# VectorE and GpSimd in program order through the whole second stage, and a verdict read back one block later

## The chip, the cores and the metric

The kernel runs on one core of a Trainium2 chip. A core has five engines that work side by side, each with its own queue of instructions: TensorE (PE, matrix multiplies), VectorE (DVE), ScalarE (ACT), GpSimd (POOL) and SyncE (SP, which issues most of the DMAs here). They wait for one another through semaphores. The metric is the device time of one execution in microseconds (us), as a median over runs; lower is better.

## The reference

A gated linear attention over 768 positions gives rows of 384 features for 3072 tokens. Two MLPs follow, and only they matter for the change:

```
x = rmsnorm(attention(q, k, v, a_re, a_im)) * rms_g     # 3072 x 384
u = silu(x @ w_gate) * (x @ w_val)                      # d_ff 1536
x = u @ w_out1                                          # 384
h = x @ w_in                                            # d_ff 2048
out = (h * clip(h + 3, 0, 6) / 6) @ w_out2              # 384
```

The inputs and outputs are 32-bit floats. The weights come as 64-bit numbers, which the kernel turns into 32-bit ones itself.

## The kernel before

Every float32 product is made of three matmuls in a reduced format: each operand is split into a high and a low part, and high x high, high x low and low x high are added in PSUM. Helper `mm3` issues them (its three lines are L735 to L737), so matmuls of all layers carry these lines, and the tile names tell them apart. VectorE makes the low parts (a subtraction), ScalarE the high parts (a copy).

**First stage** (to about 577 us). Attention and the first layer (`w_gate`, `w_val`), in units. Five engines follow an order written out by hand. The results `u` go to DRAM (`u_dr`).

**Second stage** (from about 577 us). Six blocks of 512 tokens. For each block n there are two parts:

- `o1[n]`, the product with w_out1: 12 steps j. A step fetches `uu` from DRAM (`fetch`, L898, three buffers), splits it into `uh` (ScalarE, L904) and `ul` (VectorE, L905; two buffers each) in `part`, and does 9 matmuls into the three PSUM tiles `po` (`gemm`). Three matmuls of a step need `uh` alone. After the last step `evict` copies the three `po` to `x2h` (ScalarE, L918) and makes `x2l` (VectorE, L919); both are named `x2b` in the profile.
- `m2[n]`, the second MLP: 16 steps j. `up` does 9 matmuls into one of two PSUM tiles `ph`. `act` then runs ScalarE (L948, `r`), VectorE (L949, `r`; it reads `ph` for the last time), ScalarE (L950, `gh`), VectorE (L951, `gl`). `down` does 9 matmuls into `po`, two steps behind `up`. At the end `evict` copies the three `po` to `ob`, the middle one on VectorE (L964), and SP stores them.

Beside that, the weights of the second stage are decoded tile by tile (44 tiles in all; 24 of them run beside blocks 0 and 1). Each takes four VectorE operations (L301, L303, L305 and a range check, L311, which keeps the smallest magnitude in `wmin`), one of ScalarE and one of GpSimd (L788).

The kernel is exact only for numbers in a certain range. So `recheck` reads the gate weights again (24 tiles `rawc`, two buffers, a DMA on SP each) and range-checks them (L311), and `verdict` gathers all flags with seven small VectorE operations (`okt`, `okc`), sends 128 numbers to DRAM and reads them back as one row (`okr`, two DMAs on SP, L1015 and L1016), and reduces that row to one bit (`badf`, `badi`; L1017 and L1018). At the very end the bit decides whether a slow fallback runs.

**The order.** A planner orders the instructions of each engine by a model of their times, from the program's order as priority. A `manual_schedule` context takes the named engines out of that: they keep the program's order among the instructions of the context. `manB` is such a context for VectorE and GpSimd; it opens in front of the second stage and is closed after block 0 (`o1[0]`, `o1[1]`, `m2[0]` and the decoding, merged by hand with `run`). Everything after it (blocks 1 to 5, the range checks of `recheck`, `verdict`) is ordered by the planner on all engines, and it may also mix its instructions in between those of `manB`. The loop over blocks, which emits o1[n+1] and then m2[n]:

```
for n in range(NB):
    seq = m2[n][0] + do(m2[n][1]) if n else []
    if 1 <= n and n + 1 < NB:
        seq = do(o1[n + 1][0]) + o1[n + 1][1] + do(o1[n + 1][2]) + seq
    run((seq, 0, 1), ([...recheck(i)...] if n in (1, 2) else [], 0, 1))
    if n == 3:
        verdict()
```

The two lists of a `run` are merged in proportion: in blocks 1 and 2 one recheck comes after every eleventh group of three matmuls (`up`, `down` and `gemm` each count as such groups).

Of the kernel before, what the change touches and what calls it, by code (L numbers as in the profile page):

```python
# [233 lines left out]
def attn_moe(tc, io, dbg=None):  # L234
# [580 lines left out]
    def steps_split(ns):  # L815

        out, its = [], {}
        for n in ns:
            its[n] = decode(n)
            for c in (0.0, 0.27, 0.47, 0.47, 0.47):  # L820
                out.append((c, lambda n=n: next(its[n])))
            if n - 1 in its:
                out += [(0.0, lambda n=n: list(its[n - 1]))]
        out.append((0.0, lambda: list(its[ns[-1]])))
        return out
# [3 lines left out]
    def run(*lists):  # L829

        ev = []
        for li, (lst, lo, hi) in enumerate(lists):
            tot = sum(c for c, _ in lst) or 1.0
            t = 0.0
            for i, (c, f) in enumerate(lst):
                ev.append((lo + (hi - lo) * t / tot, li, i, f))
                t += c
        for _, _, _, f in sorted(ev, key=lambda e: e[:3]):
            r = f()
            for _ in r if hasattr(r, 'send') else ():  # L840
                pass
# [91 lines left out]
    def steps_moe2(n):  # L933
# [50 lines left out]
    manB = ExitStack()  # L984
# [8 lines left out]
    o1s = lambda n: o1[n][1] + do(o1[n][2])  # L993
    run((o1[0][1], 0, 1), (do(o1[0][2]), *(1.05,1.05)), (do(o1[1][0]), 0.9, 0.9), (o1[1][1], 1, 2), (do(o1[1][2]), *(2.31,2.31)), (m2[0][0], *(1.46,4.65)), (do(m2[0][1]), 4.8, 4.8),
        (steps_split(list(range(20, len(tiles2)))), *(0.0, 3.56)))
    manB.close()

    okp = bpool("okp", bufs=1)
    okt = okp.tile([128, 11 * NU + NW], F32, name="okt")
# [5 lines left out]
    def verdict():  # L1005

        fl = lambda t, k: t[:, 0:6 * NU].rearrange("p (n k) -> p n k", k=3)[:, :, k]
        for k in range(2):
            nc.vector.tensor_scalar(out=fl(okt, k), in0=fl(flags, k), scalar1=1e15, scalar2=None, op0=ALU.is_le)
        nc.vector.tensor_scalar(out=fl(okt, 2), in0=fl(flags, 2), scalar1=2e4, scalar2=None, op0=ALU.is_le)  # L1010
        nc.vector.tensor_scalar(out=okt[:, 6 * NU:7 * NU], in0=flags[:, 6 * NU:7 * NU], scalar1=2.0 ** -40, scalar2=None, op0=ALU.is_ge)
        nc.vector.tensor_scalar(out=okt[:, 7 * NU:11 * NU], in0=flags[:, 7 * NU:], scalar1=3e38, scalar2=None, op0=ALU.is_le)
        nc.vector.tensor_scalar(out=okt[:, 11 * NU:], in0=wmin, scalar1=TINY, scalar2=None, op0=ALU.is_ge)
        nc.vector.tensor_reduce(out=okc, in_=okt, axis=mybir.AxisListType.X, op=ALU.min)
        nc.sync.dma_start(ok_dr, okc)  # L1015
        nc.sync.dma_start(okr, ok_dr.rearrange("p n -> n p"))  # L1016
        nc.vector.tensor_reduce(out=badf, in_=okr, axis=mybir.AxisListType.X, op=ALU.min)  # L1017
        nc.vector.tensor_scalar(out=badi, in0=badf, scalar1=1.0, scalar2=None, op0=ALU.is_lt)  # L1018
    def recheck(i):

        raw = okp.tile([128, DM, 2], I32, name="rawc", tag="rawc", bufs=2)
        nc.sync.dma_start(raw.rearrange("p n w -> p (n w)"), io["wgv"][:, i // 2].bitcast(I32).rearrange("p k n -> p (k n)")[:, i % 2 * 2 * DM:(i % 2 + 1) * 2 * DM])
        range_check(raw, DM, i)
# [5 lines that stand above are left out]
        run((seq, 0, 1), ([(1.0, lambda i=i: recheck(i)) for i in range(J1 * (n - 1), J1 * n)] if n in (1, 2) else [], 0, 1))  # L1029
        if n == 3:  # L1030
            verdict()
    eb.close()

    ew.close()
# [84 lines left out]
```

## Time and profile before

| | |
|---|---|
| median of 3 runs | 1148.29 us (1145.74 to 1155.37) |
| profiled execution, its own time | 1150.55 us |
| its span, first to last instruction | 1148.7 us |
| TensorE busy | 1064.4 us (93%) |
| VectorE busy | 776.8 us (68%) |
| ScalarE busy | 543.9 us (47%) |
| GpSimd busy | 73.2 us (6%) |

All rows come from the profiled execution. Busy time of TensorE is the union of its matmuls, and a matmul of 512 columns lasts about 0.39 us in the record while the next one starts about 0.23 us after it, so the starts tell more than the durations. In a timeline, brackets give the idle time of the engine before the instruction and what released it.

### The profile page before, as it was taken

The numbers are of one execution on the slowest core, as the hardware profiler recorded it, in microseconds if no ns is written. First come the engines' busy times: TensorE is split into PE (matmuls) and PEld (weight loads), VectorE is DVE, ScalarE is ACT, GpSimd is POOL, SyncE is SP. The second block draws the span as 40 slices with busy tenths as digits, with TensorE's granted clock in tenths as the row PEclk, the third lists the DMA queues.
The fourth block names the chain that finished last, engine by engine and source line by source line (L and its number), as shares of the span: only waits on it lengthen the run. The fifth ranks groups of instructions, "written<-read, shape, count | busy, mean of one in ns | idle before, by whom it ended". The sixth has DMA issues, their size and how long they took to land.

```text
span 1148.7 us, 24595 instructions
## 1 busy us (share of the span) xinstructions
PE 1064.4 (93%) x10264; PEld 926.4 (81%) x10264; DVE 776.8 (68%) x1501; ACT 543.9 (47%) x930; POOL 73.2 (6%) x99
## 2 busy tenths in 40 slices
PE   0458999999999999999999998999999999999997
PEld 0447899999999999999967886888888888888885
DVE  7999899999999987878888883432333333333332
ACT  4655667767767574623334442433332333333332
POOL 3010010000000010001222120000000000000000
PEclk9999899999999999999999999999999999999999
DMA  7526627438456365465688742200200210200000
GB/s 305 157 58 196 163 63 237 130 100 242 129 158 187 90 193 138 117 171 146 210 295 298 220 120 10 92 1 27 84 28 1 92 46 1 80 12 1 28 1 30
DMA packets 81433, 133.71 MB, mean 116 GB/s; under 512 B 32225, under 2 KB 50786, under 8 KB 80674
## 3 DMA queue, kind: packets, MB, share of 16 engines
q1 hardware_dynamic: 80658, 131.95, 38.6%
q8 instruction: 82, 1.34, 0.5%
q14 instruction: 37, 0.30, 0.1%
q10 hardware_dynamic: 656, 0.11, 0.1%
HBM read 89.77 MB, written 34.60 MB: 108 GB/s over the span
## 4 chain that ended last, share of the span: by engine, by line
PE 62%; DVE 16%; issue 8%; DMA 8%; ACT 3%; POOL 1%; SPq 1%; DVEq 0%; ACTq 0%; POOLq 0%
PE po L736 8%; PE po L737 8%; PE po L735 8%; PE pm L735 6%; PE pm L736 5%; PE pm L737 5%; PE ph L735 5%; PE ph L736 5%; PE ph L737 5%; DMA rawc<-in_wgv_dram 3%; PE psT L597 2%; PE psY L687 2%; DVE wmin L311 2%; DVE words L303 2%; DVE m L442 1%
## 5 line engine op out<-in xcount | busy, mean ns | idle before, releaser
L735 PE MATMUL pm<-xh,wg 128*128 128x256 f32 x864 | 253.7, 294 | 0.5 <-ACT xh L717 0.4
L736 PE MATMUL pm<-xl,wg 128*128 128x256 f32 x864 | 244.8, 283 | 1.8 <-DVE xl L719 1.8
L737 PE MATMUL pm<-xh,wg 128*128 128x256 f32 x864 | 244.3, 283 | 0.0
L735 PEld LDWEIGHTS pm<-xh,wg 128*128 128x128 f32 x864 | 164.4, 190 | 5.8 <-issue 0.9
L736 PEld LDWEIGHTS pm<-xl,wg 128*128 128x128 f32 x864 | 164.8, 191 | 2.3 <-DVE xl L719 2.3
L737 PEld LDWEIGHTS pm<-xh,wg 128*128 128x128 f32 x864 | 164.8, 191 | 0.1
L949 DVE SCALAR_TENSOR_TENSOR r<-r,ph 128x512 f32<-128x512 f32 x96 | 65.9, 686 | 104.0 <-ACT r L948 103.8
L951 DVE TENSOR_TENSOR gl<-r,gh 128x512 fp32r<-128x512 f32 x96 | 68.0, 708 | 94.8 <-ACT gh L950 94.5
L948 ACT ACTIVATE r<-ph,biasz 128x512 f32<-128x512 f32 x96 | 66.0, 687 | 113.1 <-PE ph L737 112.9
L736 PE MATMUL po<-gl,w_h 128*128 128x512 f32 x288 | 114.2, 397 | 4.2 <-DVE gl L951 4.2
L950 ACT ACTIVATE gh<-r 128x512 fp32r<-128x512 f32 x96 | 60.8, 633 | 113.7 <-PE po L737 87.0
L737 PE MATMUL po<-gh,w_l 128*128 128x512 f32 x288 | 114.3, 397 | 0.0
L735 PE MATMUL ph<-x2b,wi_h 128*128 128x512 f32 x288 | 113.8, 396 | 0.0
L737 PE MATMUL ph<-x2b,wi_l 128*128 128x512 f32 x288 | 113.7, 395 | 0.0
L736 PE MATMUL ph<-x2b,wi_h 128*128 128x512 f32 x288 | 113.6, 395 | 0.0
L735 PE MATMUL po<-gh,w_h 128*128 128x512 f32 x288 | 107.1, 396 | 0.0
L905 DVE TENSOR_TENSOR ul<-uu,uh 128x512 fp32r<-128x512 f32 x72 | 51.4, 714 | 73.7 <-ACT uh L904 73.6
L904 ACT ACTIVATE uh<-uu 128x512 fp32r<-128x512 f32 x72 | 45.4, 631 | 91.6 <-PE po L737 79.0
L736 PE MATMUL po<-ul,wo 128*128 128x512 f32 x216 | 85.8, 397 | 2.5 <-DVE ul L905 2.4
L737 PE MATMUL po<-uh,wo 128*128 128x512 f32 x216 | 84.9, 393 | 0.0
L603 ACT ACTIVATE XTt<-psT 112x512 f32<-112x512 f32 x96 | 55.2, 593 | 34.4 <-PE psT L597 34.0
L442 DVE TENSOR_TENSOR m<-LAt,P 128x192 f32<-128x192 f32 x192 | 68.1, 355 | 3.9 <-ACT LAt L412 0.2
(130 smaller groups left out, 1958.1 us busy)
## 6 DMA issues: line engine op xcount, KB each, us to landing
u_dr<-sg SPq DMA_DIRECT2D x72, 256.0 KB, 3.4
uu<-u_dr SPq DMA_DIRECT2D x72, 256.0 KB, 2.8
raw<-in_wo_dram SPq DMA_DIRECT2D x28, 384.0 KB, 3.6
wraw<-in_wgv_dram SPq DMA_DIRECT2D x12, 768.0 KB, 7.4
S<-in_s_all_dram SPq DMA_DIRECT2D x24, 384.0 KB, 3.8
rawc<-in_wgv_dram SPq DMA_DIRECT2D x24, 384.0 KB, 4.3
K<-k_dr SPq DMA_DIRECT2D x40, 224.0 KB, 4.3
LAt<-in_a_all_dram SPq DMA_DIRECT2D x5, 1536.0 KB, 9.0
```

The costliest lines, as they stand in the source:

```text
L303: nc.vector.scalar_tensor_tensor(out=A, in0=lo, scalar=29, in1=A, op0=ALU.logical_shift_right, op1=ALU.bitwise_or)
L442: tt(out=m4, in0=la, in1=pj, op=ALU.mult)
L603: nc.scalar.activation(d, s, AF.Copy)
L735: nc.tensor.matmul(ps, lhsT=wh, rhs=xh, start=first, stop=False)
L736: nc.tensor.matmul(ps, lhsT=wh, rhs=xl, start=False, stop=False)
L737: nc.tensor.matmul(ps, lhsT=wl, rhs=xh, start=False, stop=last)
L904: nc.scalar.activation(uh, uu, AF.Copy)
L905: (nc.gpsimd if n < 0 else nc.vector).tensor_tensor(out=ul, in0=uu, in1=uh.bitcast(F32), op=ALU.subtract)
L948: nc.scalar.activation(r, ph, AF.Relu, bias=biasz[:, 2:3], scale=sixth)
L949: stt(out=r, in0=r, scalar=1.0, in1=ph, op0=ALU.min, op1=ALU.mult)
L950: nc.scalar.activation(gh, r, AF.Copy)
L951: tt(out=gl, in0=r, in1=gh.bitcast(F32), op=ALU.subtract)
```

## The change

The context `manB` is closed only after the loop over blocks. So VectorE and GpSimd keep the program's order in blocks 1 to 5 too, with the range checks and the verdict at their place in it; TensorE, ScalarE and SyncE are still ordered by the planner. And `verdict` is cut in two: the flags are gathered and sent after block 3 as before in the program, while the reduction of the row that comes back (`verdict_end`) stands after block 4.

```diff
         (steps_split(list(range(20, len(tiles2)))), *(0.0, 3.56)))
-    manB.close()
...
         nc.sync.dma_start(ok_dr, okc)
         nc.sync.dma_start(okr, ok_dr.rearrange("p n -> n p"))
+
+    def verdict_end():
         nc.vector.tensor_reduce(out=badf, in_=okr, axis=mybir.AxisListType.X, op=ALU.min)
         nc.vector.tensor_scalar(out=badi, in0=badf, scalar1=1.0, scalar2=None, op0=ALU.is_lt)
...
         if n == 3:
             verdict()
+        if n == 4:
+            verdict_end()
+    manB.close()
     eb.close()
```

## Rows read from the trace of the kernel before

**Rows 1.** Windows of the second stage: stretch, length, busy us (instructions) by engine, clock, DMA.

```profile
577.10:611.00 33.90, 31.09 (x128) 22.67 (x127) 28.27 (x56) 13.23 (x24) 7.10 (x7) 1.00 0.90 303
611.00:658.20 47.20, 46.21 (x197) 36.48 (x196) 41.76 (x77) 19.76 (x34) 9.93 (x9) 1.00 0.80 257
658.20:692.50 34.30, 34.30 (x149) 27.57 (x148) 31.34 (x54) 14.75 (x26) 9.38 (x9) 1.00 0.38 110
692.50:701.40 8.90, 8.90 (x40) 7.19 (x39) 2.91 (x6) 2.71 (x5) 0.75 (x1) 1.00 0.73 18
701.40:710.40 9.00, 4.76 (x15) 3.45 (x14) 3.40 (x7) 1.84 (x3) 0.00 (x0) 0.81 0.08 12
710.40:1141.40 431.00, 431.00 (x1858) 348.51 (x1856) 150.64 (x222) 144.72 (x226) 0.00 (x0) 1.00 0.10 33
```

**Rows 2.** Timeline, two steps of the second MLP: start, duration, engine, line, operation.

```profile
1031.64 0.69 DVE L949 SCALAR_TENSOR_TENSOR r<-r,ph 128x512 f32<-128x512 f32 x1 [1.52 <-ACT r L948]
1035.82 0.69 DVE L949 SCALAR_TENSOR_TENSOR r<-r,ph 128x512 f32<-128x512 f32 x1 [1.50 <-ACT r L948]
```

**Rows 3.** Timeline around the verdict: SP, VectorE, TensorE.

```profile
693.67 0.33 SPq L1015 DMA_DIRECT2D ok_dr<-okc  x1
701.85 0.30 SPq L1016 DMA_DIRECT2D okr<-ok_dr  x1
705.03 0.27 DVE L1017 TENSOR_REDUCE badf<-okr 1x1 f32<-1x128 f32 x1 [9.59 <-DMA okr<-ok_dr]
705.41 0.67 DVE L951 TENSOR_TENSOR gl<-r,gh 128x512 fp32r<-128x512 f32 x1
701.50 0.40 PE L735 MATMUL po<-gh,w_h 128*128 128x512 f32 x1
706.14 0.50 PE L736 MATMUL po<-gl,w_h 128*128 128x512 f32 x1 [4.24 <-DVE gl L951]
710.59 0.39 PE L736 MATMUL ph<-x2b,wi_h 128*128 128x512 f32 x1
```

**Rows 4.** VectorE groups of 577 to 611 (first row), then timeline at 586.

```profile
L311 DVE TENSOR_REDUCE wmin<-rawc 128x1 f32<-128x384 f32 x9 | 4.9, 548 | 3.0 <-DMA rawc<-in_wgv_dram 3.0
...
585.98 0.55 DVE L311 TENSOR_REDUCE wmin<-rawc 128x1 f32<-128x384 f32 x1 [0.77 <-DMA rawc<-in_wgv_dram]
586.91 0.69 DVE L905 TENSOR_TENSOR ul<-uu,uh 128x512 fp32r<-128x512 f32 x1
587.65 0.50 PE L736 MATMUL po<-ul,wo 128*128 128x512 f32 x1 [0.52 <-DVE ul L905]
```

**Rows 5.** Timeline, the longest of the verdict's gathering operations.

```profile
692.57 0.73 DVE L1013 TENSOR_SCALAR okt<-wmin 128x68 f32<-128x68 f32 x1
```

**Rows 6.** TensorE group of 658.2 to 692.5 (one of three alike), and VectorE's timeline.

```profile
L736 PE MATMUL po<-ul,wo 128*128 128x512 f32 x15 | 5.9, 393 | 0.0
...
660.53 0.68 DVE L949 SCALAR_TENSOR_TENSOR r<-r,ph 128x512 f32<-128x512 f32 x1
691.98 0.68 DVE L949 SCALAR_TENSOR_TENSOR r<-r,ph 128x512 f32<-128x512 f32 x1
```

**Rows 7.** Timeline of TensorE, first and last of 14 matmuls put around one o1 step.

```profile
802.95 0.40 PE L735 MATMUL ph<-x2b,wi_h 128*128 128x512 f32 x1
...
808.73 0.40 PE L736 MATMUL ph<-x2b,wi_h 128*128 128x512 f32 x1
```

**Rows 8.** Timeline at the end of o1[5]: the last o1 matmul, the evictions, the next operation.

```profile
1023.70 0.39 PE L737 MATMUL po<-uh,wo 128*128 128x512 f32 x1
1023.83 1.89 DVE L919 TENSOR_TENSOR x2b<-po,x2b 128x512 fp32r<-128x512 f32 x3 [2.01 <-ACT x2b L918]
1025.63 0.68 DVE L951 TENSOR_TENSOR gl<-r,gh 128x512 fp32r<-128x512 f32 x1
```

**Rows 9.** Timeline, a gap of TensorE in the first stage, and the window around it.

```profile
551.65 0.38 PE L736 MATMUL pm<-xl,wg 128*128 128x256 f32 x1 [1.26 <-DVE xl L719]
...
550.00:560.00 10.00, 8.73 (x71) 8.54 (x72) 8.11 (x18) 3.04 (x6) 1.05 (x1) 1.00 0.81 248
```

## The prediction

> **What bounds the kernel now.** The page first: TensorE is the busiest engine. A share over stages with different limits prices nothing, so next the stretches of the second stage, from its first matmul at 577.1 us to its last at 1141.3 [rows 1]. In each, the reader compares the length with matmuls times pitch. The pitch comes from a stretch without gaps: one step of the second MLP is 18 matmuls (9 up, 9 down), and its `r` operation comes back every 35.82 - 31.64 = 4.18 us [rows 2], so 4.18/18 = 0.232 us. The stage has 6 x (108 + 288) = 2376 matmuls, 551.7 us, and took 564.4: at most 12.7 us (1.1%) can be won here. It is lost in three of the six stretches. 577.1 to 611: 33.9 - 128 x 0.232 = 4.2. 611 to 658.2: 47.2 - 197 x 0.232 = 1.5. 701.4 to 710.4: 5.5. From 710.4 on nothing is lost; matmuls fill it without a gap.
>
> Then what ended each loss. The timeline around 701 to 711 [rows 3] shows the verdict: its last reduce sat 9.59 us before it ran, waiting for a DMA that itself could be issued only 8.2 us after the first one (693.67 to 701.85). `gl` queued behind it on VectorE ran at 705.41, and TensorE stood 4.24 us for `gl`. When it ran again the granted clock fell to the lower of its two levels (1.2 GHz), 0.81 on average in this stretch [rows 1]. From 701.50 to 710.59 lie 13 matmuls: 9.09 - 13 x 0.232 = 6.1 us for the whole event. The operation groups of 577 to 611 and the timeline at 586 [rows 4] show the other loss: 9 of the 24 range checks of the gate weights were hoisted in here, took 4.9 us and waited 3.0 us for their DMA, while the splits of `ul` stood behind them (check 585.98, `ul` 586.91, matmul 587.65 late by 0.52).
>
> **Part 1, the verdict's wait (gain).** In program order the seven verdict operations come after block 3 and the two of verdict_end after block 4, some 90 us later (396 matmuls x 0.232). The readback took 8.2 us plus 3.2 (701.85 to 705.03), so verdict_end waits for nothing: -6.1 us. The seven operations now run in one burst between block 3's `ob` copy and the first `ul` of o1[5]. The longest took 0.73 [rows 5], so the burst is under 5.1. TensorE is covered by two `up` groups of m2[4], 18 x 0.232 = 4.2 us: 0 to 0.9 is left, I take 0. On SP the second DMA waits up to 8.2 us for the first, and fetches of `uu` may be queued behind it. Three `uu` buffers cover two steps of 9 x 0.232 = 2.1, leaving 0 to 4.0; whether a fetch stands there depends on the planner. I take +1.0.
>
> **Part 2, the range checks move (gain).** All 24 now stand at their place in blocks 1 and 2, one in 7.6 us (132 steps of 3 matmuls over 12). In 577 to 658 that frees on VectorE what [rows 4] shows, and the lost 5.7 us mostly go. Splits and `ul` still share VectorE there, so I keep 1.0: -4.7 (bounds -3 to -5.7). In their new place each is 0.55 us on an engine that is busy 151 of 431 us [rows 1], with 7.6 us between two for the transfer: nothing. The DMAs go along, on SP, which the change leaves free.
>
> **Part 3, m2[0] loses its filler (loss).** The manual section is the same up to m2[0], but before, automatic work of o1[2] could mix into it. From 658.2 to 692.5 TensorE was full only because 45 of its 149 matmuls were o1[2] [rows 6]. VectorE set the pace: `r` at 660.53 and, six steps on, at 691.98, 5.24 us a step where TensorE needs 4.18. Now `ul` of o1[2] may not run before m2[0] is done, so nothing fills: 6 x (5.24 - 4.18) = 6.4, less 0.5 for the `ul` that leave this stretch: +6.0. Below, 4.5 (seven `r` in the stretch, 34.3 - 0.5 us, against 7 x 4.18); above, the whole filler, 45 x 0.232 - 0.5 = 9.9.
>
> **Part 4, the end of each o1 (loss).** Blocks 1 to 4 run o1[n+1] first and m2[n] after it. On VectorE, in program order, the first `r` of m2[n] stands behind the three `x2l` of o1[n+1]. Before, the planner mixed the two: around one step of o1[3] it put 14 `up` matmuls of m2[2] (the first at 802.95, the last at 808.73) [rows 7], and it went on so to the end of o1. Two PSUM buffers for `ph` allow two `up` groups, 18 matmuls, until the first `r` is done. At 14 around one step they are spent long before o1 ends. So at the end of o1 TensorE has nothing: `up(2)` waits for `r`(0), that waits for `x2l`. The timeline at the end of o1[5] [rows 8] prices it. Last o1 matmul at 1023.70, next slot 1023.93; the three `x2l` from 1023.83 for 1.89, the next VectorE operation starts at 1025.63; `r` takes 0.69 [rows 2]; the matmul follows within 0.1: 1026.4. That is a gap of 2.45 us, four times: +9.8. If the planner holds the `up` groups back it is 0.
>
> The Trainium skill, "PSUM — Partial Sum Buffer", section "Engine vs sequencer instructions", says that VectorE's queue is strict FIFO. The trace agrees: `gl` stood behind the reduce though its own input was long there. By this rule the four gaps are there; by the full stretch after 710.4 alone they would be 0, and the sum 9.8 lower.
>
> At the start of each o1, `ul`(0) now stands behind the `ob` copy: two operations of 0.69 [rows 4], 1.4 us, against three matmuls that need `uh` alone and the `up` groups. I take 0.5 for all four (0 to 2). After 692.5 GpSimd has one operation left and after 701.4 none [rows 1]: its order costs nothing.
>
> **Sum.** -6.1 + 1.0 - 4.7 + 6.0 + 9.8 + 0.5 = +6.5 us on the profiled execution's own 1150.55, that is 1157.1. The median of the runs shown is 1148.29, 2.26 lower, so 1154.8.
>
> **Rivals.**
> A, the forecast: 1154.8.
> B, slower: the clock falls after each of the four gaps. It fell after 4.24 us of idle (6.1 less the gap from 701.73 to 706.14, 4.4: 1.7 us), and not after 1.26 us [rows 9]. 2.45 lies between the two. At 4 x 1.7 = 6.8 more it is 1161.6, slower by 1.2%. One row speaks for each side; the idle is nearer to 1.26. The Trainium skill, "Perfetto Trace Analysis", section "Matmul Optimizations", says that TensorE scales power with its utilization, so matmuls should run back to back; by it B would come true, 6.8 us above A.
> C, the gaps of part 4 do not come: the planner keeps `up` matmuls for the end of o1, as it covers every other hole after 710.4. -9.8: 1145.0. Against it: it takes whatever is ready, and 14 go around one step.
> D, the order costs nothing, in m2[0] neither: parts 1 and 2 alone, -6.1 - 4.7: 1137.5. For it: `r` in program order is how m2[0] ran up to 658 with little loss. Against it: 45 matmuls of filler have to come from somewhere.
> That the change does nothing can't be: the 9.59 us wait has its cause removed.
>
> **How the numbers follow.** A 0.38, B 0.28, C 0.22, D 0.12. The likeliest is A, with its own range, from the bounds of parts 2 and 3, of 1152 to 1160. The range of 8 in 10 runs from between D and C to past B with part 3 at its upper bound: 1139 to 1164. A measurement of this kernel can tell about 1% (11.5 us) from no change. Faster by that is under 1136.8, below all four cases: 0.03. Slower is over 1159.8: most of B, little of A: 0.22. Within 1%: 0.75.
>
> **What would show it.** No wait over 1 us on VectorE for `okr`, and no gap of 4 us on TensorE for `gl` (part 1). TensorE losing under 2 us from 577 to the end of o1[1] (part 2). TensorE idle by 0.6 to 1 us a step in m2[0] while the splits run, put down to `r` or `gl` (part 3). Four TensorE gaps near 2.45 us before an `up` matmul, each right after three `x2l`, the granted clock at 1.0 or, for B, halved behind them (part 4). I am wrong if these gaps are missing, or if in m2[0] TensorE stays full.

## The result and the profile after

The changed kernel takes 1162.36 us (median of 5, 1160.04 to 1166.34) against 1147.91 (median of 5, 1145.26 to 1155.37). The ratio is 1.0114, 95% interval 1.0078 to 1.0151: slower by 1.1%. The forecast was 1154.8; rival B (the clock falls after the four gaps) stood at 1161.6. The profiled execution took 1160.83 us, 10.3 more than that of before (1150.55), and that is the difference that the rows can account for.

Windows of TensorE in the second stage of the kernel after, which answer [rows 1]: stretch, length, busy us (matmuls), granted clock, DMA share, GB/s.

```profile
576.90:605.00 28.10, 28.10 (x125) 1.00 0.79 243
605.00:647.30 42.30, 42.30 (x185) 1.00 0.49 142
647.30:683.00 35.70, 34.30 (x144) 1.00 0.26 76
...
725.30:732.00 6.70, 4.40 (x14) 0.75 0.11 42
821.00:828.00 7.00, 4.70 (x20) 1.00 0.12 48
915.60:924.00 8.40, 6.10 (x20) 0.80 0.00 0
924.00:986.50 62.50, 62.50 (x271) 1.00 0.00 1
986.50:1006.00 19.50, 14.87 (x53) 0.82 0.65 122
1019.50:1025.00 5.50, 3.20 (x14) 1.00 0.00 0
```

A window also counts a matmul that lies across one of its ends, so these counts are one or two too high, and a loss read as length less matmuls x 0.232 comes out too low (the prediction's 4.2 and 1.5 as well). From the start of one matmul to the start of another, less 0.232 for each matmul between, nothing is lost to 647.3, where before lost 6.7. 649 to 683 loses 2.7. Around the four short stretches 3.9, 2.5, 4.0 and 2.5 are lost, 12.8 in all, and around 986.5 to 1006 it is 7.8. The long stretches between, 924 to 986.5 for one, lose nothing. From its first matmul to its last the stage takes 575.24 us, against 564.18 before.

What TensorE waited for, 576 to 1155 us, kernel after: us in total, times, longest.

```profile
PE ph L735 <- DVE r L949: 10.5, 7, 2.3
PE po L735 <- ACT uh L904: 3.8, 1, 3.8
PE po L736 <- DVE ul L905: 0.8, 1, 0.8
```

First, the four gaps. The timeline at the end of o1[2], which answers [rows 8]; three more places, at 823.74, 918.28 and 1022.00, have the same gap of 2.30:

```profile
725.18 0.39 PE L737 MATMUL po<-uh,wo 128*128 128x512 f32 x1
725.33 1.88 DVE L919 TENSOR_TENSOR x2b<-po,x2b 128x512 fp32r<-128x512 f32 x3 [1.98 <-ACT x2b L918]
727.13 0.68 DVE L949 SCALAR_TENSOR_TENSOR r<-r,ph 128x512 f32<-128x512 f32 x1
727.86 0.80 PE L735 MATMUL ph<-x2b,wi_h 128*128 128x512 f32 x1 [2.30 <-DVE r L949]
```

`r` runs straight behind the three `x2l`, with no idle time of its own: its input was there, its place in the queue was not. The matmul behind the gap lasts 0.80 instead of 0.39, the sign of the lower level of the clock; the windows show it fallen at 727 and 918 (0.75, 0.80) and not at 823 and 1022 (1.00).

Second, the verdict. Timeline from 986.9, which answers [rows 3] (SP, VectorE, ScalarE, TensorE):

```profile
986.92 0.24 DVE L1008 TENSOR_SCALAR okt<-flags 128x14 f32<-128x14 f32 x2
...
987.53 0.30 DVE L1013 TENSOR_REDUCE okc<-okt 128x1 f32<-128x145 f32 x1
...
987.90 0.45 SPq L1014 DMA_DIRECT2D ok_dr<-okc  x1
988.46 0.92 SPq L898 DMA_DIRECT2D uu<-u_dr  x2
988.49 0.50 PE L736 MATMUL po<-ul,wo 128*128 128x512 f32 x1 [0.82 <-DVE ul L905]
997.13 0.30 SPq L1015 DMA_DIRECT2D okr<-ok_dr  x1
997.36 0.63 ACT L904 ACTIVATE uh<-uu 128x512 fp32r<-128x512 f32 x1 [6.54 <-DMA uu<-u_dr]
998.04 1.65 PE L735 MATMUL po<-uh,wo 128*128 128x512 f32 x3 [3.81 <-ACT uh L904]
...
1088.43 0.26 DVE L1018 TENSOR_REDUCE badf<-okr 1x1 f32<-1x128 f32 x1
```

The reduce that waited 9.59 us before runs at 1088.43 without any idle time: the change does what it says. But in the place that the write to DRAM now has, TensorE stands 3.81 us for `uh`, and `uh` stood 6.54 for a fetch that was issued right behind that write. The view of DMA issues (KB each, median us to landing), from 987.8 to 989.5, and in the last line the DMA traffic from 992 to 998:

```profile
uu<-u_dr SPq DMA_DIRECT2D x2, 256.0 KB, 9.7
ok_dr<-okc SPq DMA_DIRECT2D x1, 0.5 KB, 9.2
...
DMA packets 74, 0.13 MB, mean 21 GB/s; under 512 B 12, under 2 KB 12, under 8 KB 74
```

Over the whole kernel a `uu` lands in 2.9 us (median). Behind the write of 128 x 4 bytes, two of them took 8.8 and 10.7, 9.7 in the middle, and all traffic from 992 to 998 came to 21 GB/s.

Third, the timeline of m2[0], which answers [rows 6]: `r` at either end of six steps, and two places between where TensorE stands for it.

```profile
649.59 0.68 DVE L949 SCALAR_TENSOR_TENSOR r<-r,ph 128x512 f32<-128x512 f32 x1
679.28 0.68 DVE L949 SCALAR_TENSOR_TENSOR r<-r,ph 128x512 f32<-128x512 f32 x1
...
660.46 0.40 PE L737 MATMUL po<-gh,w_l 128*128 128x512 f32 x1
660.99 0.50 PE L735 MATMUL ph<-x2b,wi_h 128*128 128x512 f32 x1
...
675.44 0.50 PE L735 MATMUL ph<-x2b,wi_h 128*128 128x512 f32 x1 [0.68 <-DVE r L949]
```

The range checks in their new place, a group of VectorE's from 701 to 882, which answers [rows 4] (count, busy us, mean ns, idle before):

```profile
L311 DVE TENSOR_REDUCE wmin<-rawc 128x1 f32<-128x384 f32 x24 | 13.1, 545 | 0.0
```

`r` comes every (679.28 - 649.59)/6 = 4.95 us. TensorE, which needs 4.18, first stands for it at 660.99, for 0.13 us (the matmul at 660.46 ends at 660.86), and then at 665.56, 670.33, 675.44 and 680.01; up to 660.46 it has no hole. The checks wait for nothing.

### The profile page after: what moved, and what is told of

The parts are those of the page before. It is cut to its first block, busy times and chain, and to the rows that moved or that the text cites. A ratio compares the mean times of both kernels' runs of the same rounds, so it can differ in the third digit from the quotient of the medians.

```text
span 1159.0 us, 24598 instructions
## 1 busy us (share of the span) xinstructions
PE 1069.2 (92%) x10264; PEld 931.1 (80%) x10264; DVE 775.3 (67%) x1501; ACT 545.5 (47%) x930; POOL 73.3 (6%) x99
## 4 chain that ended last, share of the span: by engine, by line
PE 74%; DVE 10%; issue 7%; DMA 4%; ACT 3%; POOL 1%; SPq 0%; DVEq 0%; ACTq 0%; POOLq 0%
PE po L735 10%; PE po L736 9%; PE po L737 9%; PE pm L735 7%; PE pm L736 6%; PE pm L737 6%; PE ph L735 6%; PE ph L736 5%; PE ph L737 5%; PE psT L597 2%; PE psY L687 2%; PE psS L650 1%; PE psU L667 1%; PE psY L678 1%; DVE X L354 1%
## 5 line engine op out<-in xcount | busy, mean ns | idle before, releaser
L735 PE MATMUL ph<-x2b,wi_h 128*128 128x512 f32 x288 | 115.7, 402 | 10.9 <-DVE r L949 10.5
L736 PE MATMUL ph<-x2b,wi_h 128*128 128x512 f32 x288 | 114.4, 397 | 0.0
L735 PE MATMUL po<-gh,w_h 128*128 128x512 f32 x288 | 103.9, 395 | 0.0
L735 PEld LDWEIGHTS ph<-x2b,wi_h 128*128 128x128 f32 x288 | 54.8, 190 | 27.6 <-DVE r L949 15.2
```

The lines of the kernel that those rows point to most:

```text
L735: nc.tensor.matmul(ps, lhsT=wh, rhs=xh, start=first, stop=False)
L736: nc.tensor.matmul(ps, lhsT=wh, rhs=xl, start=False, stop=False)
```

## The experiments

Ratios are against runs of the kernel before on the same chip, at the same time; intervals are 95%. Medians of runs that were not measured together differ by themselves: the kernel before alone has medians from 1147.91 to 1152.89. So where it says more, the length of the second stage, from its first matmul to its last in the one profile of each run, stands beside them. The first stage, at which no edit is aimed, takes between 575.0 and 580.5 us in these profiles.

### Four gaps: the place of `x2l`

The theory: the gaps come only because the first `r` of m2[n] stands behind the `x2l` of o1[n+1]. Edit of the kernel after, **e1_acts_first**: the first two groups `up`, `act` of m2[n] stand ahead of `evict` of o1[n+1].

```diff
-            seq = do(o1[n + 1][0]) + o1[n + 1][1] + do(o1[n + 1][2]) + seq
+            seq = do(o1[n + 1][0]) + o1[n + 1][1] + seq[:8] + do(o1[n + 1][2]) + seq[8:]
```

> The first two act groups of m2[n] (with their up matmuls) are moved in the program ahead of the eviction of o1[n+1]; all else as in the changed kernel. Theory O (the order on VectorE makes the gaps at the end of each o1: r(0) behind three x2l): the four TensorE gaps of 2.30 us in front of an up matmul are gone, and with them the clock falls behind two of them; 11.8 us less than the changed kernel, about 1150.5 us. Rival E (the eviction itself, or the two ph buffers whatever the order, makes the gap): four gaps of 2 us or more remain somewhere within 10 us of each o1 end, about 1162.

Measured: 1147.87 us, ratio 0.9970 (0.9942 to 0.9997), 14.5 us below the kernel after. TensorE's waits, 576 to 1145:

```profile
PE po L735 <- ACT uh L904: 4.5, 1, 4.5
PE ph L735 <- DVE r L949: 2.4, 4, 1.2
PE po L736 <- DVE ul L905: 0.8, 1, 0.8
```

No wait of 2.3 is left. The second stage takes 563.0 us, 12.2 less than in the kernel after, close to the 12.8 read there. The kernel after was not measured together with e1; the same edit between two runs that were (e2 and e5, below) gives 11.3 us. So one line of the order was worth 11 to 14 us, about the whole slowdown. The `uh` gap of the verdict is still there.

### The split, given the order

Edit of the kernel after, **e4_order_alone**: `verdict_end` right behind `verdict`.

```diff
         if n == 3:
             verdict()
-        if n == 4:
             verdict_end()
```

> The order is kept through the whole stage, but the verdict is read back at once after block 3 (the split of the verdict undone). Theory: VectorE now stands some 12 us (9.2 for the first DMA, 3 for the second) in front of the first ul of o1[5]; the 4.2 us of up matmuls cover a part, and the fetches that waited on SyncE are hidden behind it; TensorE idles some 8 to 9 us there in place of 0.8 + 3.8, so 3 to 6 us more than the changed kernel with the clock fall: about 1167. Rival (the read-back one block later is worth nothing, since SyncE stands anyway): 1162.

Measured: 1168.49 us, ratio 1.0152 (1.0120 to 1.0185). Timeline of VectorE and TensorE:

```profile
998.85 0.27 DVE L1018 TENSOR_REDUCE badf<-okr 1x1 f32<-1x128 f32 x1 [11.78 <-DMA okr<-ok_dr]
999.96 0.79 PE L736 MATMUL po<-ul,wo 128*128 128x512 f32 x1 [13.06 <-DVE ul L905]
```

The split is worth some 6 us (1168.49 against 1162.36; against e2, measured with it, 7), as expected, but only because the order by hand would have made the wait worse than the planner had it (13.06 us of TensorE here, 4.24 in [rows 3]).

### The late fetch: SP's wait, or the write itself

My first theory was that of the prediction: `uu` fetches stand behind `okr` on SP, which waits for `ok_dr`. **e2_okr_pool** issues `okr` from GpSimd; **e5_both** is that with the edit of e1.

```diff
-        nc.sync.dma_start(okr, ok_dr.rearrange("p n -> n p"))
+        nc.gpsimd.dma_start(okr, ok_dr.rearrange("p n -> n p"))
```

> The second DMA of the verdict (okr) is issued from GpSimd's queue in place of SyncE's; all else as in the changed kernel. Theory Q (SyncE stands 7.7 us for the first DMA of the verdict with the fetches of uu behind it): the TensorE gap of 3.81 us for uh near 998 and the clock fall behind it go, 6 to 7 us less than the changed kernel, about 1156. Rival S (the fetches come late there because uu's three buffers are freed late, by the burst of verdict operations on VectorE): a gap for uh of 2 us or more remains, about 1162.

> Both edits together: the first two act groups ahead of the eviction, and okr issued from GpSimd. Theories O and Q together: 18 to 19 us less than the changed kernel, about 1144, that is 4 us under the kernel before; TensorE's loss in the second stage about 4 us, nearly all of it in m2[0]. If O or Q is wrong: 1150 or 1156. If both are: 1162.

Measured: 1161.14 (ratio 1.0097, 1.0070 to 1.0123) and 1149.83 (1.0007, 0.9990 to 1.0023): nothing gained against the kernel after and e1. From e2's timeline:

```profile
997.73 0.63 ACT L904 ACTIVATE uh<-uu 128x512 fp32r<-128x512 f32 x1 [7.64 <-DMA uu<-u_dr]
997.74 0.71 POOL L1015 DMA_DIRECT2D okr<-ok_dr  x1 [317.96 <-DMA ok_dr<-okc]
998.42 1.65 PE L735 MATMUL po<-uh,wo 128*128 128x512 f32 x3 [4.91 <-ACT uh L904]
```

e2's DMA issues from 987 to 989:

```profile
uu<-u_dr SPq DMA_DIRECT2D x2, 256.0 KB, 10.6
ok_dr<-okc SPq DMA_DIRECT2D x1, 0.5 KB, 10.3
```

Here SP doesn't wait for the write to land: it issues `uu` fetches at 987.74, 988.35 and 990.85, and the gap is there all the same. The fetches were issued in time; they landed late, the first of them with the write. The theory fell. The new one (W): the write of a column of 128 x 4 bytes holds the transfers around it. Three edits of e1 test it.

**e6_pe_verdict** has no transfer at all in the verdict: the column becomes a row by a TensorE transpose.

```diff
-        nc.sync.dma_start(ok_dr, okc)
-        nc.sync.dma_start(okr, ok_dr.rearrange("p n -> n p"))
+        pt = PH["ps"].tile([128, BLK], F32, name="ph", tag="ph", bufs=2)
+        nc.tensor.transpose(pt[0:1, 0:128], okc, ident)
+        nc.scalar.activation(okr, pt[0:1, 0:128], AF.Copy)
```

> The version with the first two act groups of m2[n] ahead of o1's eviction (1147.9), in which the verdict's column okc is turned into a row by one small TensorE transpose and one ScalarE copy instead of by the write to DRAM and the read back; all is still computed. Theory W (the write of 128 x 4 bytes, which lands 9.2 us late, holds the uu fetch behind it, 8.8 to 11.4 us): the uh gap of 4.46 us, the ul gap of 0.83 and the 3.4 to 6.8 us at half clock behind them go, uu lands in about 3 us, 1147.9 - 7 = about 1141. Rival V (block 3 to block 4 is simply a place where o1[5] starts cold, its first fetches come late whatever stands before them): the uh gap stays near 4.5 us, 1148.

Measured: 1143.0, ratio 0.9949 (0.9932 to 0.9967). TensorE's waits from 570 to 1145:

```profile
PE ph L735 <- DVE r L949: 1.4, 3, 0.7
PE ph L1014 <- DVE okc L1012: 1.2, 1, 1.2
```

and the `uu` issues from 976 to 985:

```profile
uu<-u_dr SPq DMA_DIRECT2D x4, 256.0 KB, 3.0
```

The fetch is back at 3.0 us and the `uh` gap is gone, as W has it; the transpose itself makes TensorE wait 1.2. The gain shows in the second stage, 555.7 us against 563.0 of e1, 7.3 less. The medians alone don't show its size: they lie 4.9 apart, the ratios 0.9970 and 0.9949 only 2.4, on two chips and with intervals that overlap.

**e7_pool_queue** keeps both transfers and issues them from GpSimd's queue.

> The same version (1147.9) with both small transfers of the verdict issued from GpSimd's queue, so that SP neither waits nor has them in its queue. Theory W1 (the fetch is late because it stands behind the small write in the same queue): uu lands in about 3 us, no uh gap, about 1141 to 1143. Theory W2 (the small write holds the DMA engines themselves, whatever the queue): the fetch still lands 8 to 11 us after its issue and the uh gap of 4.4 us stays, 1148.

Measured: 1146.01, ratio 0.9978 (0.9951 to 1.0005). Landing times of `uu` from 970 to 995:

```profile
DMA to landing us min/median/max: 2.7/3.8/9.2
```

and TensorE's gap in the timeline:

```profile
989.57 1.65 PE L735 MATMUL po<-uh,wo 128*128 128x512 f32 x3 [2.79 <-ACT uh L904]
```

A fetch still takes 9.2 us though the write is in another queue. So W2: it isn't the order within one queue. The gap is shorter, 2.79 us against 4.46 in e1, and the second stage takes 559.8 us, between e6 and e1.

**e12_col_write** and **e13_row_write** add to e6 one write that nobody reads, 512 bytes in the middle of o1[5], as a column ([128, 1] of `okc`) and as a row ([1, 128] of `okr`).

```diff
+    x_dr = dram.tile([128, 1], F32, name="x_dr")
+    xs = okp.tile([128, 1], F32, name="xs")
+    def extra():
+        nc.vector.tensor_copy(xs, okc)
+        nc.sync.dma_start(x_dr, xs)
```

> The version with the verdict's transpose on TensorE (1143.0), with one write to DRAM that nobody reads added in the middle of o1[5], after its seventh ul: a column of 128 partitions x 4 bytes. Two uu fetches stand behind it on SP. Theory W2 (such a write holds the DMA engines for 8 to 10 us, and the fetch behind it lands late, wherever it stands): the next uu lands in 8 to 11 us instead of 2.8, TensorE stands 2 to 5 us for uh there, 1145 to 1149. Rival (the late fetch belongs to the start of o1): uu in 3 us, no gap, 1143.

> The same, with the same 512 bytes written as one row of one partition instead of a column of 128. If the 128 pieces of 4 bytes are what takes the time: the fetch behind it lands in 3 us, no gap, 1143. If any write to DRAM ahead of a fetch does it: as with the column, a fetch of 8 to 11 us and 1145 to 1149.

Measured: column 1146.01 (ratio 0.9959, 0.9940 to 0.9978), row 1143.30 (0.9938, 0.9918 to 0.9958), measured together. DMA issues at the column, from 989.6 to 994:

```profile
uu<-u_dr SPq DMA_DIRECT2D x2, 256.0 KB, 9.1
x_dr<-xs SPq DMA_DIRECT2D x1, 0.5 KB, 10.3
```

TensorE's wait behind it (985 to 1010):

```profile
PE po L735 <- ACT uh L904: 3.5, 1, 3.5
```

And the fetches around the row, from 992 to 996.5:

```profile
uu<-u_dr SPq DMA_DIRECT2D x3, 256.0 KB, 2.7
```

The second stage takes 561.4 us with the column and 555.7 with the row, as in e6. The same 512 bytes cost nothing as a row; as a column they hold a fetch for 9 us here too, and not only at the start of o1[5]. So the cause is the form of the write, a column of 128 pieces of 4 bytes; whether their number, their size or their spread over 128 partitions does it was not taken apart.

### The loss that was in the kernel before

**e8_no_rechecks** is the kernel before without its 24 range checks of the gate weights and their transfers; **e9_before_pe** is the kernel before with the transpose of e6.

```diff
-        run((seq, 0, 1), ([...recheck(i)...] if n in (1, 2) else [], 0, 1))
+        run((seq, 0, 1), ([...recheck(i)...] if n in () else [], 0, 1))
```

> The kernel before without its 24 range checks of the gate weights (they and their transfers are left out, so this part of the verdict isn't computed). By part 2 of the prediction the 9 checks hoisted to 577 to 611 us and those behind them cost 4.7 to 5.7 us: no gap before 658, about 1150.5 - 5.2 = 1145. Rival (the planner puts other work into the room and the loss comes back before 700): within 1.5 us of before, 1149 to 1152.

> The kernel before, with its own order, and the verdict's transpose on TensorE instead of through DRAM. By part 1 of the prediction the whole event at 701 to 711 (9.59 us wait on VectorE, 6.1 us lost) goes: 1150.5 - 6.1 = 1144.4. Rival (what the event covers up, a fetch or a split late in the same place, takes its room): 1148 to 1150.

Measured: 1144.99 (ratio 0.9955, 0.9929 to 0.9980) and 1143.43 (0.9943, 0.9914 to 0.9972); before, measured with them, 1149.05. So the hoisted checks cost 4.1 us and the verdict's event 5.6 by the medians; the second stage is 6.9 and 6.4 us shorter in the profiles. TensorE's waits from 570 to 1145, first without the checks,

```profile
PE po L736 <- DVE gl L951: 3.7, 1, 3.7
```

then with the transpose:

```profile
PE po L736 <- DVE ul L905: 2.6, 5, 0.8
PE ph L735 <- DVE r L949: 0.5, 1, 0.5
```

Each removes the loss that the prediction gave it and leaves the other. And e9 is as fast as e6: with the verdict mended, the planner's order and the order by hand, the latter with e1's edit, come out alike.

### The filler of m2[0]

**e10_fill_m20** is e6 with the steps of o1[2] put into m2[0] by hand (and taken out of block 1). **e11_fill_late** emits the transpose later as well.

```diff
-        (do(m2[0][1]), 4.8, 4.8),
+        (do(m2[0][1]), 4.8, 4.8), (do(o1[2][0]), 2.4, 2.4), (o1[2][1], 2.45, 4.75),
...
-            seq = do(o1[n + 1][0]) + o1[n + 1][1] + seq[:8] + do(o1[n + 1][2]) + seq[8:]
+            seq = (do(o1[n + 1][0]) + o1[n + 1][1] if n > 1 else []) + seq[:8] + do(o1[n + 1][2]) + seq[8:]
```

> The version with early act groups and the verdict's transpose on TensorE (1143.0), with the twelve steps of o1[2] put into m2[0] by hand as its filler (they stand in block 1 otherwise). Part 3 of the prediction (m2[0] runs dry on TensorE because VectorE's r comes at 4.95 us a step where 4.18 are needed, and o1[2] is the filler it lost): the three gaps before r at 660 to 676 (0.7 to 1.2 us, 2.0 to 2.3 us in all) go, r comes slower still, the stage is 2 us shorter, 1141. Rival (the twelve ul of o1[2], 0.69 us each, make VectorE later by more than the filler covers, and m2[1] without o1[2] in front of it starts with a hole): 1143 to 1147.

> The version with early act groups, transpose on TensorE and o1[2] as filler of m2[0] (1138.9), with the verdict's transpose and its ScalarE copy emitted some 47 matmuls later, inside o1[5], so that TensorE doesn't stand 1.2 us for the column okc. If that wait is on the path: the gap goes, 1138.9 - 1.2 = 1137.7. Rival (the transpose then takes a ph buffer from the up groups that stand in as filler there, and a gap for r comes instead): 1139 to 1140.

Measured: 1138.86 (ratio 0.9894, 0.9863 to 0.9924) and 1139.13 (0.9890, 0.9857 to 0.9923). e10's waits of TensorE, 570 to 1145:

```profile
PE ph L1014 <- DVE okc L1012: 1.2, 1, 1.2
PE ph L735 <- DVE r L949: 0.3, 1, 0.3
PE po L736 <- DVE ul L905: 0.2, 1, 0.2
```

The gaps for `r` at 660 to 680 are gone. The second stage takes 553.7 us against 555.7 in e6, the 2 us that were expected. The median is 4.1 below that of e6 (4.4 below e13, measured together); the rest lies in the first stage (576.1 us against 578.6 in e6's profile), and why it does isn't shown. e10 is faster than both kernels, by 1.1% than before. e11 tells nothing of its question: the planner, which still orders TensorE, put the transpose so early again that the wait of 1.2 for `okc` is in its trace as in e10's.

## Why the prediction came out as it did

The direction was right, the size 7.6 us short, and the parts were further off than the sum. By part, predicted and measured in the two profiles, from start to start:

| part | predicted | measured | from |
|---|---|---|---|
| 1, verdict | -6.1 + 1.0 | -6.1 + 7.8 | 985 to 1007 |
| 2, range checks | -4.7 | -6.7 | nothing lost to 647.3 |
| 3, m2[0] | +6.0 | +2.7 | 649 to 683 |
| 4, ends of o1 | +9.8 | +12.8 | around the four gaps |
| starts | +0.5 | +0.9 | 0.3 at 701.20, 0.6 at 1089.51 |
| sum | +6.5 | +11.4 | 11.1 between the two stages |

The executions lie 10.3 apart, since what stands outside of the stage is 0.8 us shorter in the kernel after. The 0.6 at 1089.51 isn't the start of an o1: the first `r` of m2[5] stands there behind the `ob` copy and the two operations of `verdict_end`, to which the prediction gave no price.

**Part 1 failed in one step, the +1.0.** That the wait goes was right (`badf` without idle; e9 prices the event at 5.6 us). The seven gathering operations took 0.9 us together, under the bound of 5.1. The two `up` groups that were to cover them had mostly run before, as at the ends of o1: four of their matmuls, 986.58 to 987.27, came behind the last `down`, and TensorE stood 0.82 for `ul`. The larger miss: the sentence on the three `uu` buffers ("leaving 0 to 4.0; whether a fetch stands there depends on the planner") took the fetch to be late only by its wait in SP's queue, and to land in its usual time then. The row that says otherwise was in the trace of before, unread: the landing of the one `uu` of 690 to 708, issued at 694.27 right behind `ok_dr`, in the kernel before:

```profile
DMA to landing us min/median/max: 11.1/11.1/11.1
```

TensorE's only wait there was the one for `gl`, so nothing showed it. The prediction looked at who waits in the queue and not at how long the transfer behind took. That the wait of 3.81 lies within its 0 to 4.0 is luck, since the path was another: e2 takes the wait out of SP's queue and the gap stays. The 7.8 are, from start to start, 1.0 for `ul`, 4.0 for `uh`, and 2.8 for the clock at its lower level behind them, to which the prediction gave no term here.

**Part 2 was right, and too small.** Before, all 24 checks ran between 577 and 658, not only the nine of [rows 4], 13.1 us of VectorE and 7.1 of waiting for their transfers. All of the loss came back, 6.7 from start to start, where the windows showed 5.7; the 1.0 that I kept for VectorE's other work was not needed. In their new place the checks wait for nothing (idle 0.0). e8 prices them at 4.1 by the medians and 6.9 by the second stage of the kernel before.

**Part 3 had the mechanism and the wrong size.** `r` sets the pace and TensorE stands for it, and e10, which gives the filler back, removes it. Two things in the term were off. The pace is 4.95, not 5.24 us a step, 1.76 less in six: four `ul` of o1[2], 2.7 us of VectorE, stood between the same `r` before and don't now, where I took 0.5 off. And 6 x (4.95 - 4.18) = 4.6 still isn't 2.7: TensorE has other work in hand as the stretch begins, and its first gap comes only at 660.99. I counted a slower pace as lost from its first step. The lower bound of 4.5 was built the same way and was broken too.

**Part 4 was right in place and number, and B is where A fell short.** Four gaps, each behind three `x2l`: the last o1 matmul starts at 725.18, the next slot is 725.41, and the matmul behind the gap starts at 727.86. That is 2.45, as worked out from [rows 8], and 9.8 in all (the idle time of 2.30 is shorter, since a matmul's record is longer than its pitch). VectorE's strict order, for which the Trainium skill ("PSUM — Partial Sum Buffer", section "Engine vs sequencer instructions") was named, is what the rows at 725 to 728 show, and e1 shows that it is the whole cause of the gaps. The `up` groups were indeed spent early: C didn't come.

On the clock neither A nor B is right. It fell after two of the four gaps in this profile, and 12.8 - 9.8 = 3.0 us is what that cost. The same gap of 2.30 stands four times in the profiles of e2 and e4, and the clock fell after three of four in each. So eight of twelve: about 2.7 falls in an execution where A has none and B four. A window of 10 us around such a gap holds 27 or 28 matmuls with the fall and 34 without, 7 x 0.232 = 1.6 us, near the 1.7 of B. And [rows 9] was a weak witness for A: at the same place of the first stage, near 550 us, the clock fell at a gap of 0.85 us in the profile of the kernel after and at one of 1.14 in e13's.

The median lies 14.5 us above before, the profiled executions 10.3 apart. More falls in the other executions don't explain it: three of the other four have a mean granted clock of 0.990 to 0.992, the profiled one 0.989. Part of it is the small sample: with 27, 19 and 19 runs the kernel before has medians of 1149.05, 1150.48 and 1150.88, 1 to 3 us above the 1147.91 of five. The rest stays open.

The misses cancelled in part: 6.8 too little in part 1, 3.0 in part 4 and 0.4 at the starts, against 3.3 too much in part 3 and a gain in part 2 that was 2.0 larger. That is luck. With parts 2 and 3 as predicted and the rest as measured, the time would have been some 5 us longer, above the 1164 of the range. The range held the time, near its upper end, and it did so for the gaps and the clock, not for the verdict.

## What to carry to other kernels

When a wait is moved off an engine, follow its transfers too: read, in the trace of before, how long the transfers issued just behind them took to land, even where nobody missed them. A column of 128 x 4 bytes sent to DRAM and back to turn it into a row is dear; a TensorE transpose cost 1.2 us in its place. And where two pieces of work are put one behind the other in a strict order, let the second one's first steps stand ahead of the first one's eviction: here one line of that was worth 11 to 14 us.

## What the hardware showed that was not expected

A write of 128 pieces of 4 bytes took 7.6 to 10.3 us to land, and 256 KB fetches issued behind it on SP's queue, before it had landed, took 8.6 to 11.5 instead of 2.9, and one took 9.2 when the write was in GpSimd's queue. In the kernel after even the 256 KB store issued just ahead of it took 7.9 where 2.2 is the median. As one row of 512 bytes it held nothing (2.7). The Trainium skill, "DMA: Bandwidth & Descriptors", section "Queues, rings and completion order", says that the write which marks a transfer as complete lands only after every earlier write of that DMA engine, across its queues; e7 agrees, since the fetch there was late behind another queue's write. But the rule isn't the whole of it, for the data were late too. In the kernel before, a single fetch stood behind the write: the small pieces had run by 695 (144 packets from 694 on), yet of its 0.26 MB the last 0.09 moved only between 704 and 705, and it landed at 705.38. What slows the data is open. It wasn't tried where between 4 and 512 bytes a piece the effect ends.

In the second stage TensorE's clock fell to 1.2 GHz after each of the nine idle times of 2.79 us and more (2.79, 3.46, 3.70, 3.81, 4.24, 4.41, 4.46, 4.91 and 13.06), after eight of twelve of 2.30, and after none of 1.20 or less. The length of one idle time alone doesn't decide it: in the first stage, near 550 us, the clock fell at 0.85 (kernel after) and at 1.14 (e13), and not at 1.64 (e2) and 1.75 (e4).
